# Repeated and filling matmuls in the second channel group of two long convolutions, on one Trainium2 core

## The chip, the core and the metric

The kernel runs on one core of a Trainium2 chip. A core has a matrix engine (TensorE, PE in the profile, with its weight loads as PEld), VectorE (DVE), ScalarE (ACT), GpSimd (POOL) and SyncE (SP, which here issues DMAs). Each engine has its own queue of instructions and runs it in order; engines wait for one another by semaphores. Matmul results land in PSUM and are copied from there to SBUF by DVE or ACT. The metric is the device time of one execution, in microseconds (us).

## The reference, cut to what matters

The input is a sequence of 2048 positions with 512 channels, in bfloat16. Four layers follow one another, each on a layer norm of the running sum `x`, and each added to it:

```python
x = x + A(layernorm(x))   # 32 heads; each position sees 8 earlier ones, 2 apart
x = x + B(layernorm(x))   # long convolution with a state-space kernel
x = x + A(layernorm(x))
x = x + B(layernorm(x))
```

`B` makes a kernel `K` of 2048 taps for each channel from the state-space parameters, and convolves each channel with it by FFT, both padded to 4096:

```python
Yf = rfft(pad(u)) * rfft(pad(K))
y = irfft(Yf)[:2048] + u * Dskip
```

Both `B` layers have the same parameters, so the spectrum of `K` is computed once, in the first, and kept in DRAM for the second.

## The kernel before, in words

The program first computes the taps and the first layer's projections, then the attention of layer 0 (`LayerA`), the first convolution (`FftB` with `tag` 0), the attention of layer 1, and the second convolution (`tag` 1). All is unrolled into one program.

The channels of a convolution are cut into two groups of 256 (`g` is 0 or 1, `NG` is 2), and a group into eight tiles for each step. The FFT is written as matmuls in two steps, with small tables as operands:

- `f1` (matmuls at line 720): the first step of the forward transform. Its PSUM tile is copied to `a1s` by `evac` (line 709), on ACT or DVE.
- `f2` (lines 723 to 728): the second step. One tile is 16 matmuls of 128x128 by 128x64 (line 727), each with a weight matrix of its own, into one PSUM tile. For the kernel's taps (`k_f2`) the copy goes to a spectrum buffer (line 709). For the signal (`u_f2`, lines 776 to 782) it goes to `ub`, always on ACT (line 782).
- `u_mult` (line 769): the product with the spectrum, two DVE multiplications a tile, into `t1` and `t2`. The second one reads a copy of the spectrum with swapped halves, `ks`; in the first convolution SP's DMAs make that copy (line 755), in the second a ring of buffers is loaded from DRAM (lines 759 and 761). In the first convolution, each product is followed by a DMA that stores the spectrum (line 772).
- `i1` (lines 784 to 799): the first step of the inverse. One tile is 32 matmuls of 64 rows each (line 796), which read eight channel quads of `t1` and `t2` in full, so the first tile of a group waits for all eight products of that group. The copy to `z` is at line 709. The `z` of group 0 lies in the buffer that the trace names `xnT`, since it takes over that storage.
- `i2` and `i2_rows` (lines 801 to 827): the second step, with the table `g2` (lines 821 and 822), and for ACT copies a matmul that adds `x` (line 820). DVE tiles add `x` in the copy (line 825), ACT tiles copy (line 827).

`ptile` hands out the PSUM tiles: two pools of two buffers, in pairs by turns, so that a tile takes the buffer of the fourth tile before it and waits for that one's copy.

The order of the work is written out by hand. In strings such as `ORDER0`, `ORDERF` and `ORDER1` each token emits one tile of a step: `K` and `U` are `f1` for taps and signal, `k` and `u` are `f2`, `m` is the product, `y` is `i1`, `z` is `i2`, and the letter behind names the engine of the copy. PE, DVE, ACT and SP execute in exactly this order. `FftB.run` counts the tokens, and the n-th token of a kind is tile `n % 8` of group `n // 8`. The part of the order around the change is the end of the first convolution's string and the start of the next (`ORDERF` also holds the norm and the projections with which layer 1 begins):

```python
# ORDER0, its end (u10 to u15 are group 1's f2 tiles, y0 to y2 are group 0's i1 tiles)
... u u yD yA u m yA u u m m m u u m m
# ORDERF, its start (y3 to y7, then group 1's y0 to y7, with z tiles between)
yA yA yA yA yA yA yD yA yA yA z01D yD yA yA z00A z10A z11A ...
```

In the second convolution the same steps stand in `ORDER1`, which ends the program: `... u u u m yA m yA`, then `yA m yD yD yA yD yA yA yA yD` and the `z` tiles, each followed by a store of the output.

## Time and profile before

| | |
|---|---|
| median of 3 runs | 419.25 us (419.1, 419.25, 420.06) |
| the profiled execution | 420.44 us |
| its span, first to last instruction of the program | 418.6 us |
| mean granted TensorE clock over the span | 0.981 of full speed |
| line 727 (`f2`), PE | 768 matmuls, 27.2 us busy, mean 193 ns |
| line 796 (`i1`), PE | 1024 matmuls, 40.5 us busy, mean 198 ns |
| line 782 (`ub`), ACT | 32 copies, 32.2 us busy, mean 1035 ns |
| first convolution, first `f1` tile to last `i2` tile | about 195 to 262 us |
| second convolution | about 370 to 415 us |

How to read it: a row of the profile groups instructions by line, engine and operation, with the busy time of the group and the mean duration of one. Matmuls are pipelined, so the duration of one (193 ns) is its latency, and a row of them is issued at a far shorter distance. The idle time of an engine is put down to what ended it, the releaser. The granted clock is the share of its full speed that TensorE was given; 1.00 is full speed. The windows view gives, for each stretch of time, every engine's busy time and the granted clock. The chain of waits is followed back from the last instruction, at each step to what released it.

### The profile page before, as it was taken

Reading aid. Unit: us, or ns where it says so; the run is one execution under the profiler, and the core shown is the slowest. Engines: PE = TensorE matmul, PEld = TensorE weight load, DVE = VectorE, ACT = ScalarE, POOL = GpSimd, SP = SyncE. Lnnn points to the kernel's source line nnn. Section 1 sums busy time; section 2 is a strip of 40 time slices with the busy share of each in tenths; the row PEclk is TensorE's granted clock in tenths of the full one; section 3 lists DMA queues with packets and bytes.
Section 4 is the critical chain, followed back from the end, with each engine's and each line's share of the span. In section 5 each row is a group of like instructions: output and inputs, shape, how many; then the busy total and the mean of one; then the engine's idle time right before and its main releaser. Section 6 shows DMA issues by size and latency. Waiting matters only on the chain.

```text
span 418.6 us, 15862 instructions
## 1 busy us (share of the span) xinstructions
PE 321.3 (77%) x7046; PEld 232.5 (56%) x7104; DVE 387.1 (92%) x515; ACT 323.0 (77%) x554; POOL 37.7 (9%) x46
## 2 busy tenths in 40 slices
PE   3000068999999987888998779999998978896785
PEld 2000036667756555556887668556555656666664
DVE  8999999999899999997999949979779999989995
ACT  5999998986445569997999978874555657889972
POOL 3000200000396000001400000000000020000000
PEclk9999998999999999999999969999999998999999
DMA  7940642123015666393245597730043018504506
GB/s 205 390 132 13 73 90 70 33 45 84 15 39 136 171 173 189 85 397 114 78 146 199 187 307 207 208 121 2 2 115 89 3 56 351 155 3 131 176 7 199
DMA packets 62462, 54.36 MB, mean 130 GB/s; under 512 B 33877, under 2 KB 50874, under 8 KB 61114
## 3 DMA queue, kind: packets, MB, share of 16 engines
q1 hardware_dynamic: 62250, 53.22, 42.1%
q8 instruction: 55, 0.90, 0.9%
q10 hardware_dynamic: 144, 0.13, 0.1%
q14 instruction: 13, 0.11, 0.1%
HBM read 30.28 MB, written 13.24 MB: 104 GB/s over the span
## 4 chain that ended last, share of the span: by engine, by line
PE 38%; DVE 24%; ACT 9%; DMA 7%; issue 6%; SPq 1%; DVEq 0%; ACTq 0%
DVE pav L413 8%; PE pq L359 6%; DVE a1s L709 4%; PE L L315 4%; DVE t L769 4%; PE pk L1139 4%; PE po L428 4%; PE pq L439 3%; PE pq L198 3%; DVE prod L308 3%; PE pp L255 3%; PE pp L1077 3%; DMA w_sb<-w_dram 2%; PE pb L796 2%; PE pb L821 1%
## 5 line engine op out<-in xcount | busy, mean ns | idle before, releaser
L413 DVE TENSOR_TENSOR pav<-attn,v_ext 128x4096 bf16<-128x4096 bf16 (+1 forms) x34 | 72.9, 2158 | 0.2 <-PE pq L439 0.2
L308 DVE TENSOR_TENSOR prod<-qT,kT_ext 128x4096 bf16<-128x4096 bf16 x29 | 66.0, 2300 | 3.9 <-PE L L315 3.8
L428 PE MATMUL po<-ident,pav 64*128 64x64 bf16 x2048 | 36.7, 192 | 14.2 <-DVE pav L413 8.1
L428 PEld LDWEIGHTS <-pav 64*128 64x128 bf16 x2048 | 33.2, 96 | 25.0 <-DVE pav L413 15.6
L1067 PE MATMUL pt<-ident,x_blk 128*128 128x128 bf16 x64 | 7.0, 260 | 43.4 <-ACT x_blk L171 43.4
L979 DVE TENSOR_TENSOR A_t<-A_t,pow_t 128x1024 bf16<-128x1024 bf16 (+4 forms) x46 | 38.1, 870 | 0.2
L439 PE MATMUL pq<-wop,oT 128*128 128x512 bf16 x121 | 31.6, 380 | 4.0 <-issue 3.6
L782 ACT CAST ub<-pb 128x1024 bf16<-128x1024 f32 x32 | 32.2, 1035 | 1.8 <-DVE t L769 0.8
L361 ACT CAST v_ext<-pq 128x512 bf16<-128x512 f32 x32 | 18.8, 587 | 19.2 <-PE pq L359 17.5
L727 PE MATMUL pb<-a1s,w_sb 128*128 128x64 bf16 x768 | 27.2, 193 | 6.4 <-ACT a1s L709 2.9
L315 PEld LDWEIGHTS <-prod 128*128 128x128 bf16 x928 | 27.0, 96 | 8.1 <-DVE prod L308 2.5
L1067 PEld LDWEIGHTS <-x_blk 128*128 128x128 bf16 x64 | 5.4, 117 | 46.1 <-ACT x_blk L171 44.3
L359 PE MATMUL pq<-wv,xnT 128*128 128x512 bf16 x118 | 29.9, 379 | 0.5
L709 DVE CAST a1s<-pb 128x1024 bf16<-128x1024 f32 x23 | 27.0, 1216 | 3.4 <-PE pb L720 3.4
L1077 PE MATMUL pp<-xnT,kT_ext 128*128 128x512 bf16 x87 | 24.9, 404 | 6.4 <-ACT qT L1082 3.4
L727 PEld LDWEIGHTS <-w_sb 128*128 128x128 bf16 x768 | 24.8, 98 | 8.7 <-issue 6.9
L315 PE MATMUL L<-ind,prod 128*128 128x8 bf16 x928 | 27.4, 166 | 0.8 <-DVE prod L308 0.6
L430 ACT CAST oT<-po 128x512 bf16<-128x512 f32 x32 | 18.5, 577 | 11.8 <-PE po L428 11.6
L709 ACT CAST a1s<-pb 128x1024 bf16<-128x1024 f32 x25 | 24.9, 1034 | 2.2 <-PE pb L720 1.9
L796 PE MATMUL pb<-Wp,t 64*128 64x64 bf16 x512 | 20.5, 198 | 5.9 <-ACT ub L782 3.4
L796 PEld LDWEIGHTS <-t 64*128 64x128 bf16 x1024 | 18.7, 100 | 11.0 <-issue 6.5
L1139 PEld LDWEIGHTS <-A_t 128*64 128x64 bf16 (+1 forms) x512 | 22.2, 105 | 3.6
(225 smaller groups left out, 818.9 us busy)
## 6 DMA issues: line engine op xcount, KB each, us to landing
w_sb<-w_dram SPq DMA_DIRECT2D x8, 1024.0 KB, 9.7
w_dram<-w_zero SPq DMA_DIRECT2D x1, 4096.0 KB, 14.7
kf_ring<-kf_dram SPq DMA_DIRECT2D x13, 256.0 KB, 3.9
kf_ring<-kf_dram SPq DMA_DIRECT2D x26, 128.0 KB, 4.0
v_ext<-v_ext SPq DMA_DIRECT2D x4, 784.0 KB, 6.0
x_blk<-in_A_x_dram SPq DMA_DIRECT2D x4, 512.0 KB, 4.2
kT_ext<-in_A_wqkv_dram SPq DMA_DIRECT2D x4, 512.0 KB, 10.2
x_sb<-in_A_x_dram SPq DMA_DIRECT2D x4, 512.0 KB, 5.8
```

What stands on the lines that cost most here:

```text
L308: nc.vector.tensor_tensor(pr, self.qT[q][:, ft].unsqueeze(1).to_broadcast([P, W, 4, P]), kap, ALU.mult)
L315: self.nc.tensor.matmul(L[:, al, w, ft * 8:(ft + 1) * 8], lhsT=pr[:, w, al, :], rhs=self.c["ind8"][:], start=(ft == 0 and w == 0 and al % ...
L359: nc.tensor.matmul(pp[:], lhsT=xnT[:, dt, a * P:(a + 1) * P], rhs=wv[:, dt, :], start=(dt == 0), stop=(dt == NDT - 1))
L413: nc.vector.tensor_tensor(pv[:, i], attn[:, n % 4].unsqueeze(2).to_broadcast([P, W, DH // parts, H]), vap, ALU.mult)
L428: nc.tensor.matmul(po[:, h, 0, i * nt + ft, :], lhsT=pvf[rows, i, w, ft * P:(ft + 1) * P], rhs=ident[rows, rows], start=(w == 0 and ft + i ...
L439: nc.tensor.matmul(pw[:], lhsT=oT[:, ftp, :], rhs=self.wo[:, ftp, :], start=False, stop=(ftp == NDT - 1))
L709: (self.nc.scalar.copy if eng == "act" else self.nc.vector.tensor_copy)(dst, src)
L727: nc.tensor.matmul(p2[:, j, :], lhsT=self.w2[:, ec * EC + j, :], rhs=a1s[:, ec * EC + j, :], start=True, stop=True)
L796: nc.tensor.matmul(p3[:, h, j, :], lhsT=tt[rows, dql, :], rhs=w[rows].rearrange("p m d -> p (m d)"), start=first, stop=not first)
L979: return lambda: nc.vector.tensor_tensor(*args)
L1077: nc.tensor.matmul(pps[kind, b, ft][:], lhsT=la.wqk[:, dt, c:c + P], rhs=la.xnT[:, dt, b * 512:(b + 1) * 512], start=(dt == 0), stop=(dt = ...
L1139: nc.tensor.matmul(o, lhsT=lhs, rhs=Bt[:, ri, c * CH + ql].rearrange("p b g -> p (b g)"), start=(not half and j % 4 == 0 and ri == 0), sto ...
```

## The change

Two things are added, both on PE alone, and no result changes.

First, `f2` has a new argument `again`: the first `again` of a tile's 16 matmuls are issued once more ahead of all 16, with the same operands and into the same place, which the later ones write again. `u_f2` passes `6 * g`, so the eight signal tiles of group 1 have 22 matmuls for 16, in both convolutions: 48 more matmuls, with 48 weight loads, in each. The taps' `f2` tiles are as before.

Second, `i1` issues matmuls of 128x128 by 128x512 into its PSUM tile ahead of the tile's own ones, for the first tile of group 1 alone: three in the first convolution, two in the second. They multiply the identity with a piece of the table `g2`, and the tile's own matmuls then write over them. The first of them waits for the PSUM buffer, which the tile's own first matmul waited for before, and its weight load for the DMA of `g2`; none reads `t1` or `t2`.

So PE has 101 matmuls and 101 weight loads more. The instructions of DVE, ACT, POOL and SP and their order are the same.

```diff
-    def f2(self, g, key, ec):
+    def f2(self, g, key, ec, again=0):
         nc, a1s = self.nc, self.S[g][key]
         p2 = self.ptile([P, EC, DQG])
-        for j in range(EC):
+        for j in (*range(again), *range(EC)):
             nc.tensor.matmul(p2[:, j, :], lhsT=self.w2[:, ec * EC + j, :], rhs=a1s[:, ec * EC + j, :], start=True, stop=True)
         return p2[:].rearrange("p e q -> p q e")
...
-        p2 = self.f2(g, "ua", ec)
+        p2 = self.f2(g, "ua", ec, 6 * g)
         ub = self.ub[g * NEC + ec] = self.wk.tile([P, DQG, EC], BF16, name="ub")
         nc.scalar.copy(ub[:], p2)
...
         p3 = self.ptile([P, 2, DQT, 64])
+        if t == 0 and g == NG - 1:
+            for _ in range(2 if self.tag else 3):
+                nc.tensor.matmul(p3[:, 0].rearrange("p j c -> p (j c)"), lhsT=self.ident[:],
+                                 rhs=self.g2[:, 0, 0:4, :].rearrange("p a m -> p (a m)"), start=True, stop=True)
         for j in range(DQT):
```

## Prediction

> **What bounds the kernel now.** I read the page first: TensorE (PE) is busy 77% of the span, less than VectorE (DVE, 92%), so added matmuls can be cheap. Its clock row, in fortieths of 10.5 us, matters more here.

> ```profile
> PE 321.3 (77%) x7046; PEld 232.5 (56%) x7104; DVE 387.1 (92%) x515; ACT 323.0 (77%) x554; POOL 37.7 (9%) x46
> ...
> PEclk9999998999999999999999969999999998999999
> ```

> Slice 23 (240.7 to 251.1 us) has a 6: TensorE ran there at far below its full clock. That slice is the end of the first convolution, where the changed tiles lie. Slices 6 and 33 show smaller drops. Second view: the windows view over this place. Columns: window, length, then busy time (count) of PE, PEld, DVE, ACT, POOL, then granted clock, DMA share, GB/s. I cut it where the clock changes, which the view in half-microsecond steps puts at 242.58 and 249.41.

> ```profile
> 235.75:239.17 3.42, 2.44 (x108) 2.18 (x105) 3.42 (x7) 3.20 (x4) 0.00 (x0) 1.00 0.46 163
> 239.17:242.58 3.41, 2.03 (x98) 1.57 (x95) 2.94 (x5) 3.37 (x4) 0.00 (x0) 1.00 0.63 231
> 242.58:245.99 3.41, 2.03 (x78) 2.03 (x80) 0.84 (x2) 3.23 (x4) 0.35 (x1) 0.50 0.97 360
> 245.99:249.41 3.42, 3.42 (x96) 3.02 (x91) 1.07 (x1) 2.73 (x4) 0.00 (x0) 0.50 0.98 295
> 249.41:252.82 3.41, 3.41 (x113) 2.91 (x112) 2.92 (x4) 2.00 (x3) 0.00 (x0) 1.00 1.10 366
> ```

> The clock is exactly halved for 6.83 us, two windows of 3.41. The other drops fit the same grid: 65.09 to 68.50 and 344.98 to 348.39 are one window each, and from 68.50 to 242.58 are 51 windows. So the clock is decided at the end of a 3.41 us window by what PE did in it: after 98 matmuls of the inverse tiles (L796) it fell. Third view: the same windows in the second convolution, where it stayed full with 118 and 112 matmuls nearly all of that line.

> ```profile
> 385.94:389.35 3.41, 2.11 (x66) 1.99 (x65) 3.41 (x7) 3.41 (x5) 0.00 (x0) 1.00 0.79 266
> ...
> 396.18:399.59 3.41, 2.14 (x118) 1.78 (x110) 3.41 (x7) 3.22 (x4) 0.00 (x0) 1.00 0.02 5
> 399.59:403.01 3.42, 2.15 (x112) 1.72 (x107) 3.42 (x5) 2.82 (x4) 0.00 (x0) 1.00 0.00 0
> ```

> Hence the limit, in these matmuls, lies between 98 and 112 a window. Fourth view: the chain that ended last (start, length, what), to see whether the halved clock is on the path.

> ```profile
> 239.29 3.83 DMA w_sb<-kf_sb
> ...
> 243.21 0.70 DVE t L769
> 243.92 0.04 issue
> 243.96 4.39 PE pb L796 x158
> ...
> 249.87 1.51 PE pb L796 x96
> ```

> It is. A transfer holds the last spectrum product (L769) to 243.91; then PE sets the end. 158 matmuls take 4.39 us (27.8 ns each) at half clock, 96 take 1.51 us (15.7 ns each) at full clock.

> **The change, part by part.**

> *Three fillers in the first convolution.* They stand ahead of the first inverse tile of group 1, and need only its PSUM buffer and a table loaded long before (issued at 193.2). The tile's first two matmuls start at 242.17 and then PE idles 1.59 us for the product. A 128x512 matmul costs 0.22 us (eight of L359 take 1.83 us), so three take 0.65 us and end near 242.8, 1.1 us before the product. Cost nothing; without that wait 0.65 us. Their work equals 0.65/0.0157 = 41 inverse matmuls. Some 0.4 us of it falls before the border at 242.58: 98 + 26 = 124, above the 112 that kept the clock. In the next window, at full clock, PE does 0.2 us of filler and 2.03 us of inverse work, about 140 matmuls' worth. So the fall goes.

> *What that gains.* On the chain: 158 x (27.8 - 15.7) = 1.9 us, and the eight second-stage matmuls (L821, L822) between 248.36 and 249.87 take 1.51 us where eight at 0.11 us take 0.87: 0.64 us more. Together 2.55. I also re-timed the twelve tiles from 243.96 by hand with ACT copies every 0.91 us and DVE copies of 1.22 us behind them, each tile taking the buffer of the fourth before it: with half clock this gives the z copies' end of the trace (252.88), with full clock the last of the twelve copies ends 2.6 us earlier. Next late is PE itself (x_sb tiles, then the front of layer 1, PE-bound to 277), so the gain passes on. The weights that this front needs are issued at 245.89 and 246.45 and land 7.2 us later, 253.7, against a first use at 262.0, or 259.4 after the shift.

> *48 repeated matmuls in each convolution, six per f2 tile (L727).* One costs 29 ns: 64 in a row take 2.03 us with 0.19 for the last. So 0.18 us a tile, 1.4 us a convolution.

> ```profile
> 235.24 1.56 PE L727 MATMUL pb<-a1s,w_sb 128*128 128x64 bf16 x48 [0.27 <-ACT xnT L709]
> ...
> 387.08 2.03 PE L727 MATMUL pb<-a1s,w_sb 128*128 128x64 bf16 x64 [2.67 <-ACT a1s L709]
> ```

> Cover: PE works ahead of the copies by up to four buffers. The three tiles at 235.24 end 236.80; with 18 more at 237.3, and their copies (L782) start 236.88, 238.00 and 239.21, each after its own tile. The inverse tile behind them slips from 237.07 to 237.3, and its copy is at 240.12. In the second convolution the four tiles end issuing at 389.65 instead of 389.0, and the next tile waits to 389.81 for its product anyway; the first copy there slips 0.1 us, with 0.85 us spare before DVE needs it. I take 0, bounds 0 and 2 x 1.4 = 2.8 us. Below nothing they can go too: they raise the work of the windows, so that a fall in other positions of the border is rarer or shorter. Queued behind them on PE are inverse tiles only; no DMA, DVE, ACT or SP instruction moves.

> *Two fillers in the second convolution.* 0.43 us against a hole from 400.03 to 400.57 (product's end): cost 0, bound 0.43. The clock was full there in this execution, so here they gain nothing. But a window that ended at 400.7 would hold only about 0.30 of full work against 0.36 in the one that fell. If the border lies there in other executions, they save up to one window's half, 1.7 us.

> **Sum.** The profiled execution took 420.44 us (span 418.6 and 1.84 around it): 420.44 - 2.6 = 417.8. The runs shown are 419.1, 419.25 and 420.06, two below and one near it. My hand timing offers a reason: a border after about 243.4 gives one halved window, and the loss is 1.6 us, not 2.6. If the grid starts anywhere, the runs fall in two groups 1.0 us apart, as they do. So 419.25 - 1.6 = 417.65. I take 417.7.

> [...] In the trace the longest idle time of PE before the fall at 242.58 is 0.56 us, and 1.59 us around it. [...]

> **Rivals.**

> 1. *The fall stays, or only moves.* The fillers start when the buffer is free, near 242.1. A window that ends there holds three tiles, 96 matmuls, as before, and one that ends near 244.1 holds one tile, a part of one and the fillers, again about 97. Those borders fill some 0.4 of 3.41 us, and up to a third if the limit is close to 112. Then 1.6 to 2.4 us is lost as now. If it happens in most runs: 418.3 to 419.4, within the noise. For it: the limit is known only to 98..112. Against it: the border of this profile is well covered.

> 2. *More is gained.* Before's runs may also lose clock in the second convolution (window ending 400.7; also near 387, after PE's 2.67 us idle). With 0.5 to 1 us more on the median: 416.7 to 417.2.

> 3. *Slower: PE loses its lead over the copies.* Place: the sixteen f2 tiles. If copies wait for each, 16 x 0.18 = 2.8 us come on the path, plus fillers unhidden 1.1, minus 1.6 to 2.6 of clock: 419.25 + 3.9 - 1.6 = 421.5 at worst. It decides from the point where ACT's L782 idles for L727; in 226 to 242 us its idle time is 0.4 us, none of it for PE. If the clock is halved at 387, the repeats cost 58 ns each and this is likelier.

> **How the numbers follow.** Forecast (the fall goes in most runs, the rest hidden), 417.7, from 417.2 to 418.2: 0.52. Rival 1: 0.25. Rival 2: 0.15. Rival 3: 0.08. What a measurement of this kernel can tell from no change is about 0.3%, 1.26 us, so faster is below 417.99. Faster: 0.52 x 0.85 + 0.15 and a little of rival 1 = 0.61. Slower: 0.08, and same 0.31. The range leaves out the tails of rivals 2 and 3: 416.7 to 419.3.

> **What would show it.** In the profile after: granted clock 1.00 in all windows from 235 to 256; L796 of group 1 at 15.7 ns each, with three fillers inside the wait for the last L769; L782's idle time for PE as small as now; the front of layer 1 some 2.6 us earlier. Wrong: 0.50 again in 240 to 250 (rival 1), L782 waiting on L727 (rival 3), or a full clock there with an unchanged end, which would mean that something behind 252 us takes the gain back.

## The result, and the profile after

The changed kernel takes 425.26 us (median of 6 runs, 423.44 to 429.03) against 419.49 us for the kernel before (6 runs, 418.03 to 422.25): the ratio is 1.0135, with a 95% interval of 1.0104 to 1.0166. It is slower by 5.8 us, where 1.8 us less was forecast, and outside the range. Ratios and intervals in this document leave out the runs marked slow (of before, 426.19 and 423.54 us among 29 runs on one chip), and differ by up to 0.2% from the quotient of two medians. The profiled execution took 425.46 us, with a span of 423.7 us and a mean granted clock of 0.989. Line numbers behind line 784 are four higher than before: `i1`'s matmuls are now L800, its fillers L793, the second inverse step L824 to L826, its copies L829 and L831.

First the page of after, where the last line shown is the row of a DMA queue (transfers, MB, share of 16 engines):

```profile
PE 323.4 (76%) x7145; PEld 233.4 (55%) x7205; DVE 387.2 (91%) x515; ACT 323.6 (76%) x554; POOL 37.8 (9%) x46
...
PEclk9999999999999998999999998999999999999998
...
q8 instruction: 56, 0.92, 0.9%
```

The 6 in slice 23 of the clock row is gone, as forecast, and the mean clock is higher (0.989, in before 0.981). PE has about 2 us more work and the span is 5.1 us longer. The row of q8 looks like nothing. It will turn out to be the whole matter: 0.92 MB in 56 transfers is 16.4 KB each, and 7145 + 7205 records of PE and PEld make 56 times 256 to within 14. By these counts a transfer brings 256 instructions of PE, 64 bytes each, a matmul and its weight load counting as two.

Second, the windows view of after over the end of the first convolution (columns as in the prediction):

```profile
240.22:243.64 3.42, 2.00 (x102) 1.67 (x96) 3.42 (x6) 3.23 (x5) 0.00 (x0) 1.00 0.67 243
243.64:247.05 3.41, 3.00 (x130) 2.28 (x131) 2.01 (x3) 3.41 (x5) 0.35 (x1) 1.00 1.04 381
247.05:250.46 3.41, 1.93 (x55) 1.43 (x51) 0.04 (x1) 3.14 (x4) 0.00 (x0) 1.00 0.99 296
250.46:253.88 3.42, 2.52 (x105) 2.20 (x100) 3.42 (x6) 1.93 (x2) 0.00 (x0) 1.00 1.10 344
253.88:257.29 3.41, 0.98 (x10) 0.87 (x9) 0.21 (x1) 0.46 (x1) 0.00 (x0) 1.00 1.12 207
257.29:260.70 3.41, 3.41 (x19) 2.43 (x17) 2.26 (x7) 1.57 (x2) 0.00 (x0) 0.50 0.74 229
```

The clock is 1.00 from 240 to 257. But in the fifth window PE, DVE and ACT all do next to nothing (0.98, 0.21 and 0.46 us), and in the window behind it the clock is 0.50. In before, PE is busy for the whole of that stretch:

```profile
253.88:257.29 3.41, 3.41 (x33) 3.04 (x32) 3.32 (x13) 2.37 (x3) 0.00 (x0) 1.00 1.13 254
```

What stopped PE, the chain of waits of after tells (start, length, what):

```profile
246.43 0.93 ACT z L709
...
247.39 0.42 PE pb L800 x17
247.81 1.20 issue
249.01 0.39 PE pb L800 x15
...
250.38 1.51 PE pb L800 x96
...
252.87 0.11 PE pb L826
252.98 3.33 issue
256.31 0.27 PE pb L824
```

"Issue" is time in which an engine waited for nothing that the profile shows. There are two such holes, of 1.20 and 3.33 us. The first comes in the middle of a tile, behind 17 of its 32 matmuls, where no matmul waits for anything: the operands and the buffer are those of the first 17. The second comes in the middle of a row of equal L824 to L826 triples. The waits of after (engine, line, what it waited for: us in all, times, longest) name who pays:

```profile
ACT x_sb L831 <- PE pb L826: 6.0, 4, 3.4
...
PE pb L824 <- issue: 3.3, 1, 3.3
...
PE pb L800 <- issue: 1.2, 1, 1.2
```

Third, the windows view of after, cut at the two holes:

```profile
249.01:253.00 3.99, 3.97 (x128) 3.32 (x128) 2.58 (x3) 2.71 (x4) 0.00 (x0) 1.00 1.03 338
253.00:256.30 3.30, 0.00 (x0) 0.00 (x0) 1.09 (x4) 0.39 (x1) 0.00 (x0) 1.00 1.19 228
```

Between the two holes PE executes 128 matmuls and 128 weight loads: 256 instructions, one transfer of q8. So PE stops where one piece of its instructions ends, and goes on 1.4 and 1.7 us behind the end of the next one's packets (247.60 and 254.59). In the second row the DMA share is 1.19: the times of the packets add up to more than the span of 16 engines.

**Where the 5.1 us come from.** I followed the same instruction in both traces. The last product (L769) is 0.66 us later than before, inherited from the attention of layer 0, where the two programs are still the same: this execution has a window at clock 0.50 from 158.30 to 161.72 and a hole of 0.92 us at 188.67 there, and is 1.6 us late at 193. The first DVE copy of the second step (L825, now L829) is 0.52 us later, and would be 0.7 us earlier without the hole of 1.20. The first ACT copy of that step (L827, now L831) is 4.0 us later, and the third 5.5, as the clock is 0.50 from 257.29 to 260.70, behind the window with 10 matmuls. From there on the shift hardly moves. DVE, which executes the same 515 instructions in both, is 5.5 us later from 258 to 351 us and 5.0 to 5.1 from 354 to the end. So nearly all is lost between 247 and 262 us, in the two holes and in the halved window behind them; the second convolution adds nothing.

### The profile page after: what moved, and what is told of

Same layout as the page of the kernel before. It is cut to its first block, busy times and chain, and to the rows that moved or that the text cites. A ratio compares the mean times of both kernels' runs of the same rounds, so it can differ in the third digit from the quotient of the medians.

```text
span 423.7 us, 16062 instructions
## 1 busy us (share of the span) xinstructions
PE 323.4 (76%) x7145; PEld 233.4 (55%) x7205; DVE 387.2 (91%) x515; ACT 323.6 (76%) x554; POOL 37.8 (9%) x46
## 4 chain that ended last, share of the span: by engine, by line
PE 42%; DVE 18%; ACT 11%; issue 6%; DMA 5%; SPq 1%; DVEq 0%; ACTq 0%
PE pq L359 6%; DVE pav L413 5%; PE pk L1143 5%; PE L L315 4%; DVE t L769 4%; DVE a1s L709 4%; PE pq L439 4%; PE pp L1081 4%; PE po L428 4%; PE pq L198 3%; PE pp L255 3%; DMA w_sb<-w_dram 2%; PE pb L825 2%; PE pb L826 1%; DMA kf_ring<-kf_dram 1%
## 5 line engine op out<-in xcount | busy, mean ns | idle before, releaser
L428 PE MATMUL po<-ident,pav 64*128 64x64 bf16 x2048 | 37.0, 192 | 15.0 <-DVE pav L413 7.6
L428 PEld LDWEIGHTS <-pav 64*128 64x128 bf16 x2048 | 33.3, 96 | 26.0 <-DVE pav L413 15.4
L727 PE MATMUL pb<-a1s,w_sb 128*128 128x64 bf16 x864 | 30.1, 193 | 7.0 <-ACT a1s L709 2.9
L782 ACT CAST ub<-pb 128x1024 bf16<-128x1024 f32 x32 | 32.3, 1033 | 1.6 <-DVE t L769 0.8
L727 PEld LDWEIGHTS <-w_sb 128*128 128x128 bf16 x864 | 27.6, 98 | 9.3 <-issue 7.5
L709 DVE CAST a1s<-pb 128x1024 bf16<-128x1024 f32 x23 | 27.0, 1215 | 3.5 <-PE pb L720 3.5
L359 PE MATMUL pq<-wv,xnT 128*128 128x512 bf16 x118 | 29.9, 379 | 0.5
L709 ACT CAST a1s<-pb 128x1024 bf16<-128x1024 f32 x25 | 24.9, 1034 | 2.2 <-PE pb L720 1.9
L1143 PE MATMUL pk<-B_t,A_t 128*64 128x84 bf16 (+1 forms) x512 | 23.6, 201 | 0.1
L198 PE MATMUL pq<-xnT,kT_ext 128*128 128x512 bf16 x90 | 23.0, 379 | 0.3
```

The costliest lines, as they stand in the source:

```text
L198: nc.tensor.matmul(pq[:], lhsT=self.wqk[:, dt, ft * P:(ft + 1) * P], rhs=self.xnT[:, dt, q * 512:(q + 1) * 512], start=(dt == 0), stop=(dt ...
L359: nc.tensor.matmul(pp[:], lhsT=xnT[:, dt, a * P:(a + 1) * P], rhs=wv[:, dt, :], start=(dt == 0), stop=(dt == NDT - 1))
L428: nc.tensor.matmul(po[:, h, 0, i * nt + ft, :], lhsT=pvf[rows, i, w, ft * P:(ft + 1) * P], rhs=ident[rows, rows], start=(w == 0 and ft + i ...
L709: (self.nc.scalar.copy if eng == "act" else self.nc.vector.tensor_copy)(dst, src)
L727: nc.tensor.matmul(p2[:, j, :], lhsT=self.w2[:, ec * EC + j, :], rhs=a1s[:, ec * EC + j, :], start=True, stop=True)
L1143: nc.tensor.matmul(o, lhsT=lhs, rhs=Bt[:, ri, c * CH + ql].rearrange("p b g -> p (b g)"), start=(not half and j % 4 == 0 and ri == 0), sto ...
```

## The experiments

The theory after this view is called SUPPLY in the expectations: the added instructions move the points at which pieces of PE's instruction stream end, and a piece that is asked for while the DMA engines are full comes late. Its part TRAIN names the traffic: the eight stores of the spectrum (L772) and, right behind them on SP, the weights of layer 1. The rival is WORK: the added matmuls themselves hold up PE, or the copies behind it.

What lies on the DMA engines is in the DMA view of after, 244 to 257 us (queue: packets, MB, share; then issues of one kind, KB each, us to landing), and in the timeline of SP (start, length, what it issued):

```profile
q1 hardware_dynamic: 3181, 3.96, 105.8%
q8 instruction: 2, 0.03, 1.0%
...
kT_ext<-in_A_wqkv_dram SPq DMA_DIRECT2D x2, 512.0 KB, 7.0
```

```profile
242.97 2.02 SPq L772 DMA_DIRECT2D kf_dram<-kf_nat  x4
...
246.53 0.50 SPq L227 DMA_DIRECT2D kT_ext<-in_A_wqkv_dram  x1
247.07 1.04 SPq L228 DMA_DIRECT2D kT_ext<-in_A_wqkv_dram  x1
...
248.78 2.71 SPq L281 DMA_DIRECT2D wop<-in_A_wo_dram  x4
...
```

In these 13 us two pieces of instructions (0.03 MB) come beside 3.96 MB of data. Where PE enters a piece is found by counting 128 weight loads back or on from the end of a hole. The first one's packets appear at 246.72, 1.9 us after PE entered the piece before it (244.84), and PE goes on at 249.01. The second one's appear at 253.37, 4.35 us after PE entered its predecessor (249.02), and PE goes on at 256.31. In before, with the engines at a share of 0.46 (the window from 235.75), the packets appear after 0.4 us: a piece entered at 235.82, packets of the next at 236.25. Over the whole of before and after, q8 has one packet for each entry counted like this (55 and 56), from 2.2 us ahead of it to 4.35 us behind it, with medians of 0.74 and 0.65 us behind. From this I take the fetch to be one piece ahead; no view shows it directly.

| kernel | median us | before, same chip | ratio, 95% interval | holes in the first convolution, us |
|---|---|---|---|---|
| after | 425.26 | 419.49 | 1.0135 (1.0104 to 1.0166) | 1.20, 3.33 |
| fillers alone | 419.54 | 420.26 | 0.9975 (0.9946 to 1.0005) | 0.44 |
| repeats alone | 423.55 | 420.26 | 1.0073 (1.0037 to 1.0108) | 0.52, 1.94 |
| before, 51 transposes | 426.01 | 420.26 | 1.0126 (1.0072 to 1.0181) | 1.97, 2.67 |
| before, 128 transposes | 419.79 | 420.54 | 0.9989 (0.9959 to 1.0019) | 0.84 |
| before, 90 transposes | 426.09 | 420.54 | 1.0129 (1.0079 to 1.0179) | 2.49 |
| after, 77 transposes | 423.13 | 420.26 | 1.0061 (1.0028 to 1.0095) | 0.52, 1.06 |
| after, weights held | 421.33 | 421.02 | 1.0022 (0.9988 to 1.0055) | 1.68 |
| before, weights held | 421.03 | 421.02 | 1.0002 (0.9964 to 1.0039) | none |
| fillers alone, weights held | 420.27 | 421.02 | 1.0002 (0.9971 to 1.0034) | 1.24 |
| before, 51 transposes, weights held | 423.15 | 421.02 | 1.0053 (1.0023 to 1.0082) | 1.10 |
| after, 77 transposes, weights held | 423.31 | 420.54 | 1.0069 (1.0043 to 1.0094) | 0.83 |
| one long matmul for six repeats | 421.23 | 420.57 | 1.0019 (0.9992 to 1.0046) | 0.78 |

The holes are those of the one profiled execution, above 0.3 us, from 240 to 262 us; the profile of before has none there.

### The parts alone

Fillers without repeats (6 instructions more in the first convolution, in place of 102):

```diff
-        p2 = self.f2(g, "ua", ec, 6 * g)
+        p2 = self.f2(g, "ua", ec)
```

> Only the filling matmuls, no repeats. Theory SUPPLY (PE's instructions arrive in pieces of 256, and the transfers at the end of the first convolution make a piece late; the loss depends on where the pieces end in the work): the pieces end only 6 instructions earlier in the work than in before, so the 3.3 us stall inside the second inverse step is gone or below 1 us; the clock stays full, so PE asks for pieces faster and may stall about 1 us in the first inverse step. Time 417.5 to 419.5. Theory WORK (the added matmuls themselves hold up the copies): with 5 matmuls instead of 101 nothing is held up and the clock gain is kept: 417 to 418, no stall at all.

Measured: 0.9975. The clock is 1.00 from 68 to 345 us, and the hole of 3.33 is not there. The chain of this kernel has one small hole:

```profile
249.09 0.48 PE pb L800 x25
249.57 0.45 issue
250.01 1.21 PE pb L800 x71
```

The first copy of the second step is 0.78 us earlier than in before, although the last product is 0.50 us later. Then the gain goes again: the first ACT copy of that step is 0.16 us earlier. Nor is the full clock of this execution shown to be the fillers' work: the window that ends where it fell in before (239.12 to 242.53) holds 116 matmuls, all ahead of the fillers at 243.80. Whether any gain is left in the time, the interval does not say.

Repeats without fillers (in `i1`, the filler loop goes):

```diff
-        if t == 0 and g == NG - 1:
-            for _ in range(2 if self.tag else 3):
...
```

> Only the repeats, no fillers. SUPPLY: the pieces end 96 instructions earlier in the work, nearly as in after; a stall of 2 to 3.5 us without any releaser inside the second inverse step near 253 us, at a multiple of 256 instructions from the next such stall; the clock halves near 243 as in before. Time 421 to 424. WORK: ACT's copies at line 782 idle for line 727, some 1 to 3 us in sum, and no stall without a releaser: 421 to 423.

Measured: 1.0073. Both holes are back, 0.52 us at 247.05 and 1.94 us at 251.83, again 128 weight loads apart, and the clock is halved for one window, behind one with 72 matmuls, as its windows view shows:

```profile
239.63:243.04 3.41, 1.57 (x72) 1.14 (x65) 2.90 (x6) 3.41 (x5) 0.00 (x0) 1.00 0.71 256
243.04:246.46 3.42, 3.10 (x118) 3.10 (x120) 1.49 (x2) 3.05 (x4) 0.35 (x1) 0.50 1.02 378
```

The profiled execution took 421.31 us, 2.2 us under the median of this kernel, so its holes may be smaller than usual. The repeats, then, carry the loss, and with fillers it is larger. This does not yet tell SUPPLY from WORK.

### Moving the pieces without touching the convolution

Here 51 transposes (102 instructions, as many as the change adds in the first convolution) stand at the start of the program, where PE idles (in before from 8.4 to 50.3 us), into a PSUM tile that nobody reads. The convolutions are those of before.

```diff
+        spare = pst.tile([P, 4, P], BF16, name="pt")
+        for _ in range(51):
+            nc.tensor.transpose(spare[:, 0, :], raw["C_im"][:, 0, :], ident[:])
```

> The kernel before with 51 more transposes (102 PE instructions with their weight loads) at 8 us, where PE is idle until 50 us, into a PSUM tile that nobody reads. The convolutions are untouched, but the pieces end 102 instructions earlier in their work, as in after. SUPPLY: a stall of 2 to 3.5 us in the second inverse step near 252 us, time 421 to 423. WORK, and any theory that blames the added matmuls: 419.5, as before.

Measured: 1.0126, the loss of the change. Its chain, 240 us behind the transposes (lines as in before):

```profile
245.39 0.42 PE pb L796 x17
245.81 1.97 issue
247.78 0.39 PE pb L796 x15
...
253.11 0.11 PE pb L822
253.22 2.67 issue
255.89 0.37 PE pb L820
```

The first hole comes behind 17 matmuls of the tile, as in after, and the second 128 weight loads later. WORK has nothing to say here, as the convolution has the matmuls of before. This run shows the cause: what costs is where the pieces end.

Counting weight loads from the start of the program shows it in all kernels at once. The holes of this kernel stand behind 3932 and 4060 of them, and so do the holes of after. Behind 60 us the 14 profiles of this document have 60 holes above 0.3 us put down to "issue". Divided by 128, the weight loads ahead of each leave 92, or 88 from 354 us on; a few instructions of PE that are not in this count, or missing records, would explain the step.

A whole piece of 128 transposes (256 instructions) should then change nothing, and 90 (180 instructions) should lie elsewhere.

```diff
-        for _ in range(51):
+        for _ in range(128):
```

> The kernel before with 128 transposes at 8 us, that is 256 PE instructions, one whole piece: two and a half times as many as in the run with 51, but the pieces end at the same places in the later work as in before. SUPPLY: no stall above 0.5 us near 245 to 256, and the time of before, within 0.4% (at most 1 us more from the longer idle-time work itself). Any theory by which the padding itself costs: 426 or more.

Measured: 0.9989, no difference from before. Two and a half times as many transposes as the 51 cost nothing. One hole is left, where none above 0.5 us was expected; the row of waits (236 to 264 us) has it beside PE's ordinary waits:

```profile
PE pb L796 <- ACT ub L782: 1.1, 3, 0.6
PE pb L796 <- issue: 0.8, 1, 0.8
```

```diff
-        for _ in range(51):
+        for _ in range(90):
```

> The kernel before with 90 transposes, 180 instructions: the pieces end 76 instructions later in the work than in before. SUPPLY: one end falls after about 436 of the 528 instructions of the inverse tiles' run and one after 180; the request for the second is made some 3.5 us before it is needed at half clock, against a latency of 4 us: a stall of 0.5 to 1.5 us there, the next end lies in the slow second step and costs nothing. Time 0.2 to 0.6% above before. PADDING ITSELF: between 419 and 426 in proportion, about +2%.

Measured: 1.0129, where much less was expected. The profile has a hole in the convolution, and a larger one 60 us earlier, at the end of the attention of layer 0, behind transfers of the coming convolution (issued by L1247 and L524 of this kernel up to 179.7 us; the DMA share is 0.98 from 178 to 189 us):

```profile
188.69 1.02 PE po L428 x62
189.71 2.93 issue
192.64 0.20 PE po L428 x2
```

I had thought of the convolution alone. The attention has the same weak place, and its matmuls (L428) are as short (mean 192 ns in before, L796 198). Its holes also differ from one execution to another where nothing was moved: the eight kernels without transposes have the same instructions and the same piece ends up to there, and their holes between 140 and 195 us sum to 0.5 us (repeats alone) up to 4.3 us (one long matmul). So the size of a hole in one profile says little on its own, and the medians decide.

The same lever on the changed kernel: 77 transposes fill 102 + 154 to 256 instructions, so that the pieces behind the change end where they did in before.

```diff
+        for _ in range(77):
+            nc.tensor.transpose(spare[:, 0, :], raw["C_im"][:, 0, :], ident[:])
```

> The kernel after with 77 such transposes at 8 us: 102 + 154 = 256 instructions, so the pieces end at the same place in the work behind the added matmuls as in before. SUPPLY: the 3.3 us stall goes, one of about 1 us may stay, the clock stays full: 417 to 419. WORK: the same as after, 425.

Measured: 1.0061. The hole of 3.33 is gone and less than half of the loss is left, but a gain over before was expected and did not come. The pieces between the transposes and the convolution are now shifted by 154 instructions, and a hole of 1.06 us stands at 151.04 in the attention, followed by a halved window at 151.9. In the convolution 0.52 and 1.06 us are left.

### Clearing the DMA engines

The weights of layer 1 are held back: a DVE write of one element into their tile stands behind the first copy of the second step, and the first transfer waits for it, with the others behind it on SP.

```diff
-yA yA yA yA yA yA yD yA yA yA z01D yD ...
+yA yA yA yA yA yA yD yA yA yA z01D H yD ...
...
-    la.front_w()
...
+        def hold():
+            nc.vector.memset(la.wqk[0:1, 0, D:D + 1], 0.0)
+            la.front_w()
```

> The kernel after, with the weight transfers of layer 1 (about 3 MB, issued by SP from 246.5 us on) held until the first second-step tile has been copied: one 1x1 memset on DVE that the first of them has to wait for. Theory TRAIN (a piece of PE's instructions is late since it queues among these transfers): the 3.3 us stall shrinks below 1 us, the clock does not fall, the time comes down from 425 to 418 to 420. Theory RATE (PE runs out because it consumes 256 short instructions faster than any piece can come, transfers or not): the stall stays above 2 us, 424 to 426.

Measured: 1.0022. SP now issues the first of them at 251.62, and its timeline ahead of that has nothing behind the last store:

```profile
244.93 0.65 SPq L772 DMA_DIRECT2D kf_dram<-kf_sb  x1
251.62 0.39 SPq L227 DMA_DIRECT2D kT_ext<-in_A_wqkv_dram  x1
```

The chain of this kernel keeps the first hole, which lies behind the stores, and has none where the second one was. The weight load 128 behind the one at 248.07 starts at 253.43, and PE runs through:

```profile
245.97 0.42 PE pb L800 x17
246.39 1.68 issue
248.07 0.39 PE pb L800 x15
...
250.26 2.24 PE pb L800 x96
...
253.27 0.11 PE pb L824
253.38 0.11 PE pb L825
253.49 0.11 PE pb L826
```

The packets of that piece come at 249.10, 1.0 us after PE entered its predecessor, and 4.3 us before they are needed. So the transfers of layer 1's weights make the second piece late, with the same instructions: TRAIN holds for it. The 96 matmuls take 2.24 us, as the clock is 0.50 from 248.45 to 251.86, behind the hole. That gives the piece more time, but is not what saves it. At the pace of after PE would need it at 252.06 (3.99 us after entry). Its packets end at 250.03, and with the 1.7 us that PE took behind their end in after it could go on at 251.7. In after they had only appeared 0.4 us after PE ran out.

RATE is not empty, though. Repeats alone has a small hole in the second convolution too, 0.38 us at 400.26, with a DMA share of 0.02. PE entered that piece at 397.19, ran out 3.07 us later and went on 3.45 us after entry. So short matmuls outran a piece at a DMA share of 0.02 as well; at 1.0 to 1.2 PE went on later, 4.2 and 7.3 us after entry in after.

The same hold on before, on fillers alone, and on before with 51 transposes:

> The kernel before with the same hold. Its pieces end at places where it hardly stalls, so both theories expect no change: 419 to 420.5. If the held weights came too late for the front of layer 1, 1 to 3 us more.

> Fillers only, with the same hold. TRAIN: the clock gain of 1.6 to 2.6 us is no longer partly eaten by a late piece: 417 to 418.5, the fastest of all. RATE: as fillers only, 419.5.

> The kernel before with the 51 transposes at 8 us (426 without the hold, stalls of 1.97 and 2.67 us) and the hold. TRAIN: 420 to 421.5, the second stall gone, the first smaller. RATE: 425 to 426.

Measured: 1.0002, 1.0002 and 1.0053. Held weights alone gain and cost nothing, so what they took from after was the hole. With the 51 transposes, 1.0126 becomes 1.0053 and the second hole goes, as in after. The miss is the second: fillers with the weights held were to beat before, and have a hole of 1.24 us at 250.80 and stalls of 1.62, 1.23 and 0.92 us in the attention of layer 0, whose code is before's.

Both remedies together:

> The kernel after with both remedies: 77 transposes (pieces end as in before) and the held weights. SUPPLY with TRAIN: below the run with the padding alone and below the one with the hold alone, 0 to 0.4% above before, since a stall of 0.5 to 1.5 us in the first inverse step and the shifted ends in the first attention stay. If both remedies act on something else, no better than either.

Measured: 1.0069, no better than 77 transposes alone. A hole of 0.83 us is left in the convolution and one of 1.36 us at 151.12 in the attention, with halved windows between 152 and 166. The remedies don't add. That the transposes moved a hole into the attention would explain it, but is not shown: before with the weights held has no transposes, and has a hole of 1.71 us at 153.79, behind 1500 weight loads, as this one.

### The same work in fewer instructions

Six repeats of 64 columns are replaced by one matmul over 512 columns, ahead of the tile's own: about the same PE time, 2 instructions for 12. The fillers stay.

```diff
-        for j in (*range(again), *range(EC)):
+        if again:
+            nc.tensor.matmul(p2[:, 0:8, :], lhsT=self.w2[:, ec * EC, :], rhs=a1s[:, ec * EC:ec * EC + 8, :], start=True, stop=True)
+        for j in range(EC):
```

> The kernel after, with the six repeats of a tile replaced by one matmul of 128x512 into the same PSUM tile: 0.22 us of PE instead of 0.18, so no less work and no less activity for the clock, but 2 instructions instead of 12. The pieces then end 22 instructions earlier in the first convolution's end than in before, not 102. SUPPLY: the 3.3 us stall goes (its place needs a shift near 100), one of 0.5 to 1.5 us in the first inverse step stays: 0 to +0.4% of before. WORK: as after, +1.3%.

Measured: 1.0019, the interval holds 1. Its chain has one hole of 0.78 us (L802 is `i1` in this kernel), and no second:

```profile
248.54 0.37 PE pb L802 x17
248.90 0.78 issue
249.69 1.32 PE pb L802 x79
```

WORK expects the loss of the change here, as PE does as much. It falls.

## Why the prediction was wrong

**What bounds the kernel: right as far as the runs show it.** The clock fell to 0.50 behind thin windows: 98 matmuls in before, 72 with repeats alone, 10 in after. "Granted clock 1.00 in all windows from 235 to 256" came true in after. But the profile does not show that the fillers did it. After's border lies at 243.64, ahead of the fillers (243.73), and the window before it holds 102 matmuls of its own. Both kernels with 51 and 128 transposes kept the clock there with no filler. The fillers can be seen to matter in one place, with the long matmul: its window 241.43 to 244.84 holds 88 matmuls and the three fillers, fewer than the 98 that fell, and kept the clock. Where the border falls differs from execution to execution (242.58 in before, 243.64 in after, 243.04 with repeats alone), which rival 1 had priced. The forecast's shares of full work, 0.30 in a window that ends at 400.7 and 0.36 in the one that fell, were estimates of mine; the windows view of before counts 90 matmuls (397.29 to 400.70) and 98.

**The fillers fit: right.** They start at 243.73, when the buffer is free, and end at 244.54; the last product ends at 244.57. They come 1.5 us later than forecast, since ACT was 1.6 us late from the attention, and still lie in the wait.

**What the clock gains: too large.** 2.6 us were forecast. Measured on the first copy of the second step, against the last product and without the hole, it is 1.3 us in after (0.52 - 0.66 - 1.20), 1.3 us with fillers alone (-0.78 - 0.50) and 1.9 us with the long matmul (-1.33 - 0.56). With the clock full, the chain of after lies on ACT's copies (L709) from 241.84 to 247.35, not on PE.

**The repeats at nothing: this step failed, though not by its rival.** The forecast took "0, bounds 0 and 2 x 1.4 = 2.8 us" from their time on PE. Alone they cost 0.73% (0.37 to 1.08%), some 3.1 us. Their time on PE is hidden, as forecast: from 228 to 244 us ACT's copies (L782) idle 0.2 us, for a product of DVE and never for L727. Rival 3 stood on that wait, and it does not come. What the step left out is that an instruction is also something to be fetched, through q8 in transfers of 16.4 KB. 48 repeats and 3 fillers are 102 instructions, so each later piece ends 102 instructions earlier in the work, and PE at full clock used up 256 short ones in 4.0 us (249.01 to 253.00).

**"So the gain passes on": failed.** Behind 252 PE was to be the next bound. It was, and it stood still for want of instructions: 3.33 us. In before both pieces came in time. PE entered a piece at 245.67 and needed the next 4.5 us later, at half clock; it entered that one at 250.19 and needed the next 7.9 us later, since fewer matmuls lie there. In after PE ran out 3.0 and 4.0 us after entry, and went on 4.2 and 7.3 us after it. For the first hole the halved clock of before had hidden this: fillers alone (6 instructions apart) and 128 transposes have before's piece ends and a full clock there, and a hole of 0.44 and 0.84 us. They have no second hole. That one comes with the shift, at either clock: 3.33 us in after, and 2.67 us with 51 transposes, where the clock is halved from 248.95 to 252.37. The prediction's third sign of being wrong, "a full clock there with an unchanged end", was of this kind, but I had priced nothing for it.

**What the views could have shown.** The row of q8 was on the page, and stalls put down to "issue" in rows of equal matmuls were in the trace of before (0.66 us at 165.27, in the attention). The 128 weight loads between the holes of after give the piece: 256 instructions. At a DMA share of 1.0 to 1.2 its crossing left holes of 1.20 and 3.33 us, at a share of 0.02 one of 0.38 us.

**What stays open.** Where in the fetch the time goes (waiting to be asked for, or its packets behind others) was not taken apart. In after the packets appeared 1.9 and 4.35 us after entry, took 0.9 and 1.2 us, and PE went on 1.4 and 1.7 us behind their end. So the second piece's longer delay lies mostly ahead of its packets. The first hole differs from kernel to kernel (0.4 to 2.0 us) in part because PE runs out at different times: 3.0 us after entry in after, 3.9 with fillers alone, 2.5 with 51 transposes, while it goes on after 4.2, 4.4 and 4.5 us. Whether the fillers alone gain is not settled. Holding the spectrum's stores back as well wasn't tried, so that they make the first piece later than the 3.45 us above is argued from their place, not shown. No version tried is clearly faster than before.

## What to carry to other kernels

Count added instructions as well as their time: here a small matmul and its weight load were two of 256 in a piece of PE's instructions, and 51 transposes moved the piece ends 240 us behind them, at a cost of 1.26%. Where rows of short matmuls run at full clock while DMA engines are full (here 128 in 3.99 us, at a share of 1.03), look for holes put down to "issue" in mid-tile, check whether multiples of 128 weight loads lie between them, and then move traffic (here 1.0135 became 1.0022), or do the same work in fewer and longer matmuls (1.0019). A pad in idle time tells cheaply whether a slowdown is one of position: pad by part of a piece and by a whole one (here 1.0126 and 0.9989).
